# Zero writes moved to the routing, the row's owner word stored with the row, and an earlier schedule for weights, gathers and scaling in a two-network mixture-of-experts kernel

## The chip, the cores and the metric

The kernel runs on one core of one Trainium2 chip. The metric is the device time of one execution in microseconds (us). The engines are TensorE (PE, with its weight loads as PEld), VectorE (DVE), ScalarE (ACT), GpSimd (POOL) and SyncE (SP); SP, ACT and POOL issue DMA transfers, which run on 16 DMA engines.

## What is computed

A two-dimensional Fourier transform over 8 x 3072 tokens of 256 columns, of which the real part is kept; then a mixture of 8 experts whose weights P come from eight Sinkhorn iterations over all tokens; then a second mixture in which each token goes to its best expert alone.

```python
X = np.fft.fft(np.fft.fft(x, axis=1), axis=2).real          # (8, 3072, 256), then flattened
P = np.exp(logits - logits.max())                           # logits = X @ w_gate
for _ in range(8):
    P /= P.sum(1, keepdims=True) + 1e-09
    P /= P.sum(0, keepdims=True) + 1e-09
    P *= N / E
out = sum(P[:, e:e+1] * (np.maximum(X @ w1[e], 0) @ w2[e]) for e in range(8))
# second mixture: expert_idx = argmax(out @ w_gate2), its softmax weight, the same two layers
```

## The kernel before

Most tokens have a weight of zero for every expert after the exponential, so the kernel computes only the (token, expert) pairs that count. After the transform, a routing step (`route1`) finds them, sorts them into 30 tiles of 128 rows and gives each row's source index `R["hidx"]` and output row `R["ow"]`. Each of the 8 experts (e0 to e7) has CAP = 3 tiles of its own (t = 3e to 3e+2); NFLAT = 6 "free" tiles f0 to f5 hold what overflows, and one of them is computed in each of e2 to e7 with weights gathered per row (`Free.weights`: fw, the first layer, with rawc and gd, the second layer and gate). The rows are gathered from H by GpSimd, three gathers to a block (`grab`, L1335), ten blocks: one for each expert and two (8 and 9) for the free tiles. Between two gathers of blocks after the first two stand two memsets of a small tile, which space them.

Every product is done with each operand split into a high part and a low part: `part` (L813) has ScalarE copy a weight's high part (w1h, w2h) and VectorE subtract it for the low part (w1l, w2l); `relu` does the same for the hidden layer (hh, hl), `turn` (L840) for the transposed input (xh, xl). `build` in `moe1` (L1581) makes an expert's input x from the gathered rows in four steps a to d, with a, c and d on VectorE and b on ScalarE.

The order of the work is written by hand. `experts` walks through e0 to e7. In each there are slots: 0 to 7 after the eight pieces of the first layer, 8 to 10 in the free tile's second layer (from e2 on), 11 after the transposes of the next x, and 12 to 20, three in each of the second layer's tiles. Tables at L1431 to L1457 put pieces of other work into the slots: BUILD and FBUILD the steps a to d, PART the weight splits, ZERO the zero writes of the output (`zeros(2)` is one transfer of 512 KB), LOGIT the gate logits of a gathered block, GRAB1 the gathers, FREE the free weights, and SINK with STEPS the 18 Sinkhorn steps (start; eight times rows and column sums; end), where the k-th entry is counted in slots from SINK on. Each engine takes its instructions in that program order. The column sums are one matmul on TensorE (L999), which waits for the row step on VectorE. At the last step the weights are known: `add` then scales the stored tiles y and writes them to the accumulator `acc`, and `send` scatters with addition the rows that belong to another tile's owner; ADDS and SENDS give their slots. Before the weights are known, y is kept unscaled; at the end `ask` reads the second gate's logits back from acc.

Loads of whole weights go through three buffers rawa, rawb and rawc on SyncE's queue, in the order of the list FETCH; a load waits until the buffer's last reader is done, and what stands behind it on SyncE waits too. `fill` (L1310) places gate matmuls and other work inside `route1`; the string table G2 holds its letters: g a half of one expert's gate matmuls, l the write of L, digits the first splits, w a warming matmul. `azero` (L1612) writes zeros to the first rows of acc and then the output-row words, the column DG of acc.

Of the kernel before, what the change touches and what calls it, by code (L numbers as in the profile page):

```python
# [7 lines left out]
F32 = mybir.dt.float32  # L8
# [3 lines left out]
AF = mybir.ActivationFunctionType  # L12
# [1014 lines left out]
def dense(tc, ctx, A, K, rt, R, Ld, H, Pd, out, wg2):  # L1027
# [69 lines left out]
    with tc.For_i(0, NT, 1) as i:  # L1097
# [17 lines left out]
        for s in range(2):  # L1115
# [26 lines left out]
FETCH = [("t", 0, "a"), ("t", 1, "b"), ("t", 2, "c"), ("t", 3, "1"), ("t", 4, "2"), ("t", 5, "2"), ("w1", 0, "a"), ("w2", 0, "b"),  # L1142
         ("t", 6, "c"), ("t", 7, "a"), ("w2", 1, "b"), ("w1", 1, "a")]
FETCH += [(w, e, b) for e in range(2, E) for w, b in (("w1", "a"), ("w2", "b"))]
# [5 lines left out]
def run(tc, ctx, A, out, H, acc, Ld, Pd, Gd, Zd):  # L1150
# [62 lines left out]
    with tc.manual_schedule():  # L1213
# [27 lines left out]
        with ExitStack() as st:  # L1241
# [53 lines left out]
            with ExitStack() as s1:  # L1295
# [14 lines left out]
                def fill(k):  # L1310

                    def f():
                        for c in G2[k]:
                            if c == "g":
                                e, q = half.pop(0)
                                gates2(e, [q])
                            elif c == "l":
                                nc.sync.dma_start(out=Ld, in_=L.rearrange("p t s e -> p (t s e)"))
                            elif c == "w":
                                warm(1)  # L1320
                            else:
                                part("w", 0, int(c), nc.vector, lows[int(c) // 2])
                    return f
# [11 lines left out]
                def grab(j):  # L1335
                    X[j] = xg.tile([128, CAP, HW], F32, name="Xg")
                    for i in range(CAP):
                        t = CAP * j + i
                        if j > 1:

                            for _ in range(2):
                                nc.gpsimd.memset(grow, 0.0)
                        gather(nc, X[j][:, i], H[0:12296], R["hidx"][:, t:t + 1])
# [94 lines left out]
ONP, ONQ, ONB = [], [(7, 5)], ()  # L1438
FREE = {"w": 5, "u": 2}

BUILD = [(5, 7, 7, 11), (0, 1, 2, 3), (1, 2, 3, 4), (0, 1, 2, 3), (0, 1, 2, 3), (1, 2, 3, 4), (3, 4, 4, 5), (1, 2, 3, 4)]
FBUILD = ((1, (11, 12, 14, 15), 0), (4, (11, 12, 12, 15), 0))
ZERO = [(4, 11, 15), (4, 11, 16), (4, 11, 16), (4, 11, 16), (2, 11, 16), (2, 11, 16), (2, 11, 16), (2,)]
LOGIT = ((0, 11), (0, 11), (0, 13), (0, 19), (1, 3), (1, 7), (1, 14), (1, 19), (0, 16), (2, 3))

GRAB1 = ((0, 0, 2), (0, 5, E), (0, 13, 3), (0, 18, 4), (1, 2, 5), (1, 7, 6), (1, 15, 7), (1, 20, E + 1))
SINK = (2, 4)
STEPS = [0, 0, 4, 4, 8, 8, 12, 12, 16, 16, 20, 20, 24, 24, 28, 28, 32, 33]
FIRST = 7
ADDS, SENDS = (1, 3, 5, 7, 9, 13, 14, 15, 17, 19), (7, 13, 16, 19)  # L1450

GRAB = ((0, 17, 4), (1, 4, 5), (2, 4, 9), (2, 14, 6), (3, 13, 7))
PROB = ((0, 4, 0), (0, 1, 1), (1, 11, 8), (2, 6, 2), (3, 4, 3), (4, 4, 4), (4, 11, 9), (5, 4, 5), (6, 4, 6), (7, 5, 7))
BACK, BF, BL = [(8,), (8,), (8,), (8,), (4, 8), (2, 4, 6, 8)], ((2, 9), (4, 9), (6, 9)), 10
G2 = ("gg", "", "gggggg", "0l12g3gg", "ggww", "ggg")
Y2 = (8, 9)
# [86 lines left out]
class Free:  # L1543
# [5 lines left out]

    def weights(self, f):  # L1550
        moe = self.moe
        for i in range(2 + (self.Gd is not None)):
            if i < 2:
                t = (moe.fp, moe.raw)[i].tile([128, 2, FF], F32, name=("fw", "rawc")[i])
                d = t.rearrange("p k f -> p (k f)")
            else:
                t = moe.fp.tile([128, 8, 8], F32, name="gd")
                d = t.rearrange("p a b -> p (a b)")
            gather(self.nc, d, self.src[i], self.R["frow"][:, f:f + 1])
            self.w[f, i] = t  # L1560
# [14 lines left out]
def moe1(nc, K, R, acc, moe, W, part, X, xg, Gd, w1f, w2f, xb, pt, zeros, zt, rest, ask, trash, warm, grow):  # L1575
# [35 lines left out]

    def azero():  # L1612

        ow = xb.tile([128, NTL + 1], F32, name="ow")
        o.cp(ow[:, 0:1], trash)
        o.cp(ow[:, 1:NFLAT + 1], R["ow"][:, E * CAP:])
        o.cp(ow[:, NFLAT + 1:], R["ow"][:, :E * CAP])
        n = (NFLAT + 1) * DW
        av = acc[:n // DW * 128].rearrange("(p a) d -> p (a d)", p=128)
        for c in range(0, n, 512):  # L1620
            w = min(512, n - c)
            nc.sync.dma_start(out=av[:, c:c + w], in_=zt[:, 0, :w])
        nc.sync.dma_start(out=acc.rearrange("(t p) c -> p t c", p=128)[:, :, DG], in_=ow)

# [3 lines left out]
    def keep(t, p):  # L1628
        y = late["y"].tile([128, DW], F32, name="y")
        if not alone(t):  # L1630
            G.memset(y[:, DG:], 0.0)
        nc.scalar.activation(out=y[:, :DG], in_=p, func=AF.Copy, **({"scale": R["wt"][:, t:t + 1]} if known[0] else {}))
        ys.append((t, y, p if known[0] else None))

    def add():

        if ys:
# [3 lines left out]
            if t < E * CAP:  # L1641
                r = row_tile(t) * 128
                late["q"].dma_start(out=acc[r:r + 128, :DG], in_=y[:, :DG])
                if not alone(t):
# [30 lines left out]
    for (e, at, g), j in zip(FBUILD, (E, E + 1)):  # L1675
        for s, f in zip(at, build(j, G if g else V)):
            sl.at(e, s, f)
    sl.at(0, 14, azero)
    for e, s, j in GRAB1:
# [30 lines left out]
    for f in range(NFLAT):  # L1710
        sl.at(F0 + f - 1, FREE["w"], lambda f=f: free.weights(f))
    turned, steps = experts(moe, W, "w", xt, lambda j: (lambda i: x[j][:, i]), sl, DG, keep, part, free, on, grow)
# [104 lines left out]
```

## Time and profile before

| | |
|---|---|
| median of 3 runs | 688.7 us (684.64 to 691.24) |
| profiled execution, its own time | 690.08 us |
| its span | 687.8 us |
| TensorE, VectorE, ScalarE, GpSimd busy | 636.7, 435.5, 323.9, 216.2 us |
| mean granted TensorE clock | 0.953 |

A row of a timeline gives the start and the length in us, the engine, the line, the operation, output<-input, and in brackets the idle time of that engine just before it with what ended the wait. Equal neighbours are merged, with their number behind an x. A row of a stretch gives the busy time of each engine in it, the granted clock of TensorE (1.00 is 2.4 GHz, 0.50 is 1.2 GHz), the busy share of the 16 DMA engines and the GB/s that they moved. Busy times count overlapping instructions once; an idle engine that is not the bottleneck costs nothing.

### The profile page before, as it was taken

The page shows a single profiled execution, that of the slowest core. Times are in us where ns is not written, and L with a number is a line of the kernel's source. Part 1 is how long each engine was busy: PE and PEld are TensorE (multiplying, and loading weights), DVE is VectorE, ACT ScalarE, POOL GpSimd, SP SyncE. Part 2 cuts the span into 40 slices and gives each one's busy share as a digit, 9 for nine tenths or more (in the row PEclk, how much of TensorE's full clock was granted, in tenths as well). Part 3 has the DMA queues.
Part 4 walks back from the last instruction along what each step waited for, and adds up shares of the span by engine and source line. Part 5 has one row for each costly group of instructions (what it writes and reads, how often), then busy time and mean ns, then how long its engine had stood idle before and what let it go on. Part 6 is the DMA issues. An engine that isn't in the chain of part 4 may idle for free. (4 is left out here: it accounts for less than half of the span.)

```text
span 687.8 us, 12757 instructions
## 1 busy us (share of the span) xinstructions
PE 636.7 (93%) x4835; PEld 612.8 (89%) x4835; DVE 435.5 (63%) x973; ACT 323.9 (47%) x696; POOL 216.2 (31%) x343
## 2 busy tenths in 40 slices
PE   9999999999998997996969896998799999999995
PEld 6889999999988996995959896997499999999995
DVE  3677877777238956759896671855466546745750
ACT  3444545555545213553434571763145555654651
POOL 0002221122110088821011513402367676332232
PEclk9989999999999779898989998999899999999999
DMA  8999998999889148897547879776654385457501
GB/s 212 274 220 289 258 292 271 271 294 298 305 294 372 63 130 277 304 236 282 184 156 188 248 198 363 201 255 190 198 195 167 116 307 220 181 190 262 207 24 35
DMA packets 63840, 155.24 MB, mean 226 GB/s; under 512 B 14788, under 2 KB 32588, under 8 KB 55965
## 3 DMA queue, kind: packets, MB, share of 16 engines
q1 hardware_dynamic: 53612, 114.54, 53.5%
q0 software_dynamic: 9840, 39.45, 17.9%
q8 instruction: 40, 0.66, 0.4%
q10 hardware_dynamic: 320, 0.37, 0.2%
q14 instruction: 28, 0.22, 0.1%
HBM read 103.90 MB, written 50.34 MB: 224 GB/s over the span
## 5 line engine op out<-in xcount | busy, mean ns | idle before, releaser
L431 DVE SCALAR_TENSOR_TENSOR hl<-ph,hh 128x384 fp32r<-128x384 f32 (+1 forms) x164 | 86.0, 543 | 105.7 <-ACT hh L880 105.3
L927 PE MATMUL py<-w2h,hh 128*128 128x264 f32 (+1 forms) x480 | 140.4, 292 | 0.0
L927 PE MATMUL py<-w2l,hh 128*128 128x264 f32 (+1 forms) x480 | 137.7, 287 | 0.0
L927 PE MATMUL py<-w2h,hl 128*128 128x264 f32 (+1 forms) x480 | 137.5, 287 | 0.0
L880 ACT ACTIVATE hh<-ph 128x384 fp32r<-128x384 f32 (+1 forms) x164 | 76.7, 481 | 60.8 <-PE ph L940 33.3
L927 PEld LDWEIGHTS py<-w2l,hh 128*128 128x128 f32 x480 | 93.0, 194 | 0.2 <-DVE w2l L832 0.2
L927 PEld LDWEIGHTS py<-w2h,hh 128*128 128x128 f32 x480 | 93.0, 194 | 0.0
L927 PEld LDWEIGHTS py<-w2h,hl 128*128 128x128 f32 x480 | 92.5, 193 | 0.0
L894 PE MATMUL ph<-xh,w1h 128*128 128x384 f32 x256 | 67.6, 345 | 1.1 <-DVE nf L426 0.9
L894 PE MATMUL ph<-xl,w1h 128*128 128x384 f32 x256 | 65.2, 335 | 0.0
L894 PE MATMUL ph<-xh,w1l 128*128 128x384 f32 x256 | 65.1, 335 | 0.0
L126 POOL TENSOR_TENSOR lc<-hd 128x32 f32<-128x32 f32 (+1 forms) x25 | 9.5, 381 | 167.6 <-ACT hd L122 149.8
L74 PE MATMUL pp<-ca,w 96*128 96x96 f32 x512 | 61.5, 279 | 0.0
L74 PEld LDWEIGHTS pp<-ca,w 96*128 96x128 f32 x512 | 60.4, 196 | 0.8 <-issue 0.3
L801 POOL DMA_INDIRECT out_dram<-y,Rorow x30 | 33.2, 1108 | 82.0 <-ACT hh L880 26.9
L940 PE MATMUL ph<-Xg,fw 128*128 128x128 f32 x384 | 47.3, 283 | 7.2 <-DMA fw<-in_w_dram,Rfrow 7.2
L940 PEld LDWEIGHTS ph<-Xg,fw 128*128 128x128 f32 x384 | 46.0, 199 | 7.6 <-DMA fw<-in_w_dram,Rfrow 5.6
L894 PEld LDWEIGHTS ph<-xh,w1h 128*128 128x128 f32 x256 | 45.4, 189 | 3.4 <-DVE nf L426 1.2
L91 PE MATMUL pp<-cb,t 128*128 128x128 f32 x368 | 47.5, 276 | 0.6 <-DVE t L84 0.6
L76 ACT ACTIVATE at<-pp 128x384 f32<-128x384 f32 x64 | 31.1, 492 | 33.3 <-PE pp L74 32.8
L894 PEld LDWEIGHTS ph<-xh,w1l 128*128 128x128 f32 x256 | 46.4, 188 | 0.0
L894 PEld LDWEIGHTS ph<-xl,w1h 128*128 128x128 f32 x256 | 46.3, 188 | 0.0
(332 smaller groups left out, 1266.2 us busy)
## 6 DMA issues: line engine op xcount, KB each, us to landing
out_dram<-zt SPq DMA_DIRECT2D x48, 512.0 KB
H<-hd SPq DMA_DIRECT2D x24, 562.0 KB
xa<-in_xa_dram SPq DMA_DIRECT2D x32, 384.0 KB
xm<-in_xm_dram SPq DMA_DIRECT2D x32, 384.0 KB
rawa<-in_w_dram SPq DMA_DIRECT2D x8, 1024.0 KB
rawb<-in_w_dram SPq DMA_DIRECT2D x8, 1024.0 KB
rawa<-in_u_dram SPq DMA_DIRECT2D x8, 1024.0 KB
rawb<-in_u_dram SPq DMA_DIRECT2D x8, 1024.0 KB
```

Source lines behind the costliest of these rows:

```text
L74: nc.tensor.matmul(p[:M, i], lhs(4 * h + i), ca, start=True, stop=True)
L76: nc.scalar.activation(out=at[:M, :, :, s0:s0 + 4], in_=p[:M].rearrange("m s g j -> m g j s"), func=AF.Copy)
L91: nc.tensor.matmul(p[:M, i * 128:(i + 1) * 128], t[:, i, :M], cb[:, (g0 + i) * 128:(g0 + i + 1) * 128], start=True, stop=True)
L126: nc.gpsimd.tensor_tensor(out=lc[:np_, :n], in0=hd[:np_, :, 129:137], in1=hd[:np_, :, 273:281], op=ALU.add)
L431: self.nc.vector.scalar_tensor_tensor(out, a, s, b, op0, op1)
L801: nc.gpsimd.indirect_dma_start(out=dst, out_offset=bass.IndirectOffsetOnAxis(ap=idx, axis=0), in_=src, in_offset=None, **kw)
L880: self.nc.scalar.activation(out=a[:, :n], in_=p[:, :n], func=AF.Relu)
L894: self.nc.tensor.matmul(p[:, :N], w, xx, start=(i == 0), stop=(i == 5))
L927: self.nc.tensor.matmul(p[:, :nd], c, W[2 + m // 4][w][:, m % 4, :nd], start=(m == 0 and i == 0), stop=(m == 7 and i == 2))
L940: self.nc.tensor.matmul(p[:, m * 128:(m + 1) * 128], w[:, k, (m0 + m) * 128:(m0 + m + 1) * 128], x[:, k, i * 128:(i + 1) * 128], start=(k ...
```

## The change

The output's zeros that e0 and e1 wrote (six transfers of 512 KB) and the zeros of acc are issued inside the routing, with a new letter z in `fill`. `azero` becomes `owners`, which writes the output-row words of 8 tiles only; the other tiles carry the word in column DG of y, put there by ScalarE in `keep`, and store it with the row. The first weight of e1 is loaded ahead of its second. Gathers of blocks 2 to 9 are no longer spaced by memsets and stand in earlier slots. The free weight's first layer is gathered in slot 1, the other two pieces stay in slot 5. The Sinkhorn steps begin in slot 13 of e1 and have five slots for each iteration; LOGIT follows. The sends stand in slots 7, 10, 13 and 16.

```diff
-         ("t", 6, "c"), ("t", 7, "a"), ("w2", 1, "b"), ("w1", 1, "a")]
+         ("t", 6, "c"), ("t", 7, "a"), ("w1", 1, "a"), ("w2", 1, "b")]
...
+                            elif c == "z":
+                                for _ in range(6):
+                                    zeros(2)
+                                n = (NFLAT + 1) * DW
+                                av = acc[:n // DW * 128].rearrange("(p a) d -> p (a d)", p=128)
+                                for a in range(0, n, 512):
+                                    w = min(512, n - a)
+                                    nc.sync.dma_start(out=av[:, a:a + w], in_=zt[:, 0, :w])
...
-                        if j > 1:
-
-                            for _ in range(2):
-                                nc.gpsimd.memset(grow, 0.0)
                         gather(nc, X[j][:, i], H[0:12296], R["hidx"][:, t:t + 1])
...
-FREE = {"w": 5, "u": 2}
+FREE = {"w": (1, 5), "u": 2}
-BUILD = [(5, 7, 7, 11), (0, 1, 2, 3), (1, 2, 3, 4), ...
+BUILD = [(5, 6, 6, 6), (0, 1, 2, 3), (1, 2, 3, 4), ...
-ZERO = [(4, 11, 15), (4, 11, 16), (4, 11, 16), (4, 11, 16), (2, 11, 16), (2, 11, 16), (2, 11, 16), (2,)]
-LOGIT = ((0, 11), (0, 11), (0, 13), (0, 19), (1, 3), (1, 7), (1, 14), (1, 19), (0, 16), (2, 3))
-GRAB1 = ((0, 0, 2), (0, 5, E), (0, 13, 3), (0, 18, 4), (1, 2, 5), (1, 7, 6), (1, 15, 7), (1, 20, E + 1))
-SINK = (2, 4)
-STEPS = [0, 0, 4, 4, 8, 8, 12, 12, 16, 16, 20, 20, 24, 24, 28, 28, 32, 33]
+ZERO = [(), (), (4, 11, 16), (4, 11, 16), (2, 11, 16), (2, 11, 16), (2, 11, 16), (2,)]
+LOGIT = ((0, 11), (0, 11), (0, 13), (0, 19), (1, 1), (1, 3), (1, 5), (1, 7), (0, 16), (1, 12))
+GRAB1 = ((0, 0, 2), (0, 2, E), (0, 5, 3), (0, 7, 4), (0, 13, 5), (0, 16, 6), (0, 19, 7), (1, 1, E + 1))
+SINK = (1, 13)
+STEPS = [0, 1, 8, 8, 13, 13, 18, 18, 23, 23, 28, 28, 33, 33, 38, 38, 43, 44]
-ADDS, SENDS = (1, 3, 5, 7, 9, 13, 14, 15, 17, 19), (7, 13, 16, 19)
+ADDS, SENDS = (1, 3, 5, 7, 9, 13, 14, 15, 17, 19), (7, 10, 13, 16)
-G2 = ("gg", "", "gggggg", "0l12g3gg", "ggww", "ggg")
+G2 = ("gg", "", "gggggg", "0lz12g3gg", "ggww", "ggg")
...
-    def azero():
-        ow = xb.tile([128, NTL + 1], F32, name="ow")
+    def owners():
+        ow = xb.tile([128, E], F32, name="ow")
         o.cp(ow[:, 0:1], trash)
-        o.cp(ow[:, 1:NFLAT + 1], R["ow"][:, E * CAP:])
-        o.cp(ow[:, NFLAT + 1:], R["ow"][:, :E * CAP])
...
+        o.cp(ow[:, 1:], R["ow"][:, CAP:E * CAP:CAP])
+        av = acc.rearrange("(t p) c -> p t c", p=128)[:, :, DG]
+        r = row_tile(CAP)
+        nc.sync.dma_start(out=av[:, 0:1], in_=ow[:, 0:1])
+        nc.sync.dma_start(out=av[:, r:r + CAP * (E - 1):CAP], in_=ow[:, 1:])
...
-        if not alone(t):
+        if t < E * CAP and not alone(t):
             G.memset(y[:, DG:], 0.0)
+        else:
+            nc.scalar.activation(out=y[:, DG:], in_=R["ow"][:, t:t + 1], func=AF.Copy)
...
-                late["q"].dma_start(out=acc[r:r + 128, :DG], in_=y[:, :DG])
+                w = DW if alone(t) else DG
+                late["q"].dma_start(out=acc[r:r + 128, :w], in_=y[:, :w])
...
-    sl.at(0, 14, azero)
+    sl.at(0, 14, owners)
...
-        sl.at(F0 + f - 1, FREE["w"], lambda f=f: free.weights(f))
+        sl.at(F0 + f - 1, FREE["w"][0], lambda f=f: free.weights(f, (0,)))
+        sl.at(F0 + f - 1, FREE["w"][1], lambda f=f: free.weights(f, (1, 2)))
```

## Rows read from the trace of the kernel before

**Rows 1.** The page: the span, and each engine's busy time.

```profile
span 687.8 us, 12757 instructions
PE 636.7 (93%) x4835; PEld 612.8 (89%) x4835; DVE 435.5 (63%) x973; ACT 323.9 (47%) x696; POOL 216.2 (31%) x343
```

**Rows 2.** Busy time by stretch: e2 and e3 (PE, PEld, DVE, ACT, POOL, clock, DMA, GB/s).

```profile
299.40:333.30 33.90, 27.38 (x192) 26.96 (x190) 27.41 (x70) 14.58 (x31) 3.04 (x5) 0.90 0.78 265
333.30:367.80 34.50, 27.93 (x194) 27.12 (x193) 29.51 (x75) 14.24 (x30) 3.12 (x5) 0.90 0.61 196
```

**Rows 3.** Timeline of TensorE, 250 to 430 us: instructions with idle time before them.

```profile
273.97 0.90 PE L847 MATMUL pt<-ident,x 128*128 128x128 f32 x3 [4.28 <-DVE x L1584]
...
319.03 0.60 PE L999 MATMUL pt<-cs,tri 128*128 128x8 f32 x2 [6.50 <-DVE cs L437]
347.77 0.39 PE L999 MATMUL pt<-cs,tri 128*128 128x8 f32 x2 [2.01 <-DVE cs L437]
353.31 0.55 PE L847 MATMUL pt<-ident,x 128*128 128x128 f32 x3 [1.80 <-DVE cs L428]
356.62 0.59 PE L999 MATMUL pt<-cs,tri 128*128 128x8 f32 x2 [2.76 <-DVE xl L422]
394.95 3.81 PE L940 MATMUL ph<-Xg,fw 128*128 128x128 f32 x32 [1.75 <-DMA fw<-in_w_dram,Rfrow]
424.79 5.84 PE L940 MATMUL ph<-Xg,fw 128*128 128x128 f32 x32 [5.43 <-DMA fw<-in_w_dram,Rfrow]
```

**Rows 4.** After the wait in e0: one stretch, and e1's first matmul.

```profile
274.00:278.00 4.00, 4.00 (x19) 4.00 (x20) 3.86 (x20) 0.57 (x2) 3.18 (x6) 0.50 0.59 95
...
279.46 0.52 PE L894 MATMUL ph<-xh,w1h 128*128 128x384 f32 x2
```

**Rows 5.** The chain that ended last: start, length, what; two pieces at full clock.

```profile
438.96 2.91 PE py L927 x24
...
536.90 3.57 PE ph L940 x32
```

**Rows 6.** Timelines of SyncE and ScalarE: e1's first weight, issued and used.

```profile
259.17 0.52 SPq L1210 DMA_DIRECT2D rawa<-in_w_dram  x1
...
271.13 2.00 ACT L824 ACTIVATE w1h<-rawa 128x1024 fp32r<-128x1024 f32 x2 [6.18 <-DMA rawa<-in_w_dram]
```

**Rows 7.** Timeline of VectorE, e2: a logits step's end, start's first, row step's last.

```profile
309.49 0.19 DVE L422 TENSOR_TENSOR P<-P,sg__3013 128x24 f32<-128x24 f32 x1
...
314.23 0.28 DVE L434 COPY vp<-Rvalid 128x24 f32<-128x24 f32 x2
...
318.40 0.58 DVE L437 TENSOR_REDUCE cs<-P 128x8 f32<-128x240 f32 x1
```

**Rows 8.** Timelines of VectorE and TensorE in e1: the build of block 8.

```profile
281.31 0.56 DVE L431 SCALAR_TENSOR_TENSOR hl<-ph,hh 128x384 fp32r<-128x384 f32 x1 [2.96 <-ACT hh L880]
...
294.29 0.55 DVE L1584 TENSOR_TENSOR Xg<-Xg 128x381 f32<-128x381 f32 x1
...
294.09 0.52 PE L874 MATMUL pt<-ident,Xg 128*128 128x128 f32 x3
```

**Rows 9.** Timeline of GpSimd: first and seventh scatter; the chain: the gather behind.

```profile
372.21 1.62 POOL L801 DMA_INDIRECT acc<-y,Rapos  x1 [25.70 <-DMA acc<-y]
...
412.63 1.55 POOL L801 DMA_INDIRECT acc<-y,Rapos  x1 [3.43 <-ACT w1h L824]
...
414.48 10.26 DMA fw<-in_w_dram,Rfrow
```

**Rows 10.** A stretch of the routing, columns as in rows 2.

```profile
226.00:238.00 12.00, 11.52 (x101) 10.88 (x100) 11.79 (x16) 2.65 (x6) 0.00 (x0) 0.85 0.01 3
```

**Rows 11.** Timelines of GpSimd and VectorE: the third gather, its use, the spacing memsets.

```profile
243.49 0.95 POOL L796 DMA_INDIRECT Xg<-H,Rhidx  x1 [0.30 <-issue]
...
247.04 0.30 DVE L1584 TENSOR_TENSOR Xg<-Xg 128x33 f32<-128x33 f32 x2 [0.60 <-DMA Xg<-H,Rhidx]
...
250.17 0.66 POOL L1342 MEMSET grow<- 8x256 f32 x2
```

More of the change, by code (lines that the diff above doesn't have):

```diff
@@ L1438 @@
 ONP, ONQ, ONB = [], [(7, 5)], ()
-FREE = {"w": 5, "u": 2}
-BUILD = [(5, 7, 7, 11), (0, 1, 2, 3), (1, 2, 3, 4), (0, 1, 2, 3), (0, 1, 2, 3), (1, 2, 3, 4), (3, 4, 4, 5), (1, 2, 3, 4)]
+FREE = {"w": (1, 5), "u": 2}
+BUILD = [(5, 6, 6, 6), (0, 1, 2, 3), (1, 2, 3, 4), (0, 1, 2, 3), (0, 1, 2, 3), (1, 2, 3, 4), (3, 4, 4, 5), (1, 2, 3, 4)]
 FBUILD = ((1, (11, 12, 14, 15), 0), (4, (11, 12, 12, 15), 0))
-ZERO = [(4, 11, 15), (4, 11, 16), (4, 11, 16), (4, 11, 16), (2, 11, 16), (2, 11, 16), (2, 11, 16), (2,)]
-LOGIT = ((0, 11), (0, 11), (0, 13), (0, 19), (1, 3), (1, 7), (1, 14), (1, 19), (0, 16), (2, 3))
-GRAB1 = ((0, 0, 2), (0, 5, E), (0, 13, 3), (0, 18, 4), (1, 2, 5), (1, 7, 6), (1, 15, 7), (1, 20, E + 1))
-SINK = (2, 4)
-STEPS = [0, 0, 4, 4, 8, 8, 12, 12, 16, 16, 20, 20, 24, 24, 28, 28, 32, 33]
+ZERO = [(), (), (4, 11, 16), (4, 11, 16), (2, 11, 16), (2, 11, 16), (2, 11, 16), (2,)]
[3 more added lines that the diff above has]
+STEPS = [0, 1, 8, 8, 13, 13, 18, 18, 23, 23, 28, 28, 33, 33, 38, 38, 43, 44]
 FIRST = 7
-ADDS, SENDS = (1, 3, 5, 7, 9, 13, 14, 15, 17, 19), (7, 13, 16, 19)
+ADDS, SENDS = (1, 3, 5, 7, 9, 13, 14, 15, 17, 19), (7, 10, 13, 16)
 GRAB = ((0, 17, 4), (1, 4, 5), (2, 4, 9), (2, 14, 6), (3, 13, 7))
@@ L1548, in __init__, with weights @@
         self.w, self.w2, self.x = {}, {}, {}
-    def weights(self, f):
+    def weights(self, f, pieces=(0, 1, 2)):
         moe = self.moe
-        for i in range(2 + (self.Gd is not None)):
+        for i in pieces[:len(pieces) if self.Gd is not None else 2]:
             if i < 2:
@@ L1609, in build @@
         return [a, b, c, d]
-    def azero():
-        ow = xb.tile([128, NTL + 1], F32, name="ow")
+    def owners():
+        ow = xb.tile([128, E], F32, name="ow")
         o.cp(ow[:, 0:1], trash)
-        o.cp(ow[:, 1:NFLAT + 1], R["ow"][:, E * CAP:])
-        o.cp(ow[:, NFLAT + 1:], R["ow"][:, :E * CAP])
[L1618 to L1623, printed above, removed]
+        o.cp(ow[:, 1:], R["ow"][:, CAP:E * CAP:CAP])
[3 more added lines that the diff above has]
+        nc.sync.dma_start(out=av[:, r:r + CAP * (E - 1):CAP], in_=ow[:, 1:])
     ys, sq, known, late = [], [], [False], {"q": nc.sync}
```

## The prediction

> **What bounds the kernel now.** I read the page first. The profiled execution spans 687.8 us and took 690.08 us, 2.3 us lying around the span; TensorE is busy for 93% of it and VectorE for 63% [rows 1]. So the kernel is bound by TensorE where TensorE is fed, and a change is worth what it takes from TensorE's waits. The change touches the routing and the first expert network, so the next view is the busy time by expert (e0 to e7): e2 takes 33.9 us and e3 34.5 us, while TensorE works 27.4 and 27.9 us in them and VectorE 27.4 and 29.5 us [rows 2]. VectorE has as much to do there as TensorE, so any order in which one waits for the other costs time. Then TensorE's own list of idle times says which wait ends last where [rows 3]. In e0 it stands 4.28 us for the tile x of e1, which VectorE builds. In e2 and e3 it stands four times, 6.50 + 2.01 + 1.80 + 2.76 = 13.1 us, for VectorE's Sinkhorn steps and what is queued around them (three of the four are the column-sum matmul of line 999). At the start of e5 and e6 it stands 1.75 and 5.43 us for a free tile's gathered weight fw. Together that is 24.5 us.
>
> A wait costs more than itself. After the 4.28 us wait the granted clock is 0.50 [rows 4], the lower of its two levels, and from 273.97 to 279.46 us TensorE needs 5.49 us for three transposes and 24 matmuls [rows 3, 4]. 24 such matmuls take 2.91 us at the full clock [rows 5], three transposes about 0.3, so 2.25 us more are lost. After the 5.43 us wait, 32 matmuls of line 940 take 5.84 us [rows 3] against 3.57 at the full clock [rows 5], so 2.27. I use 2.25 us for a drop of the clock. In e2 and e3 the mean clock is 0.90 each [rows 2]: one drop in each.
>
> **Part A, e0: weight order and build slots.** VectorE is late for x because it stands in program order behind the split of e1's first weight (w1l), and that behind ScalarE's w1h, which sat 6.18 us until the load landed at 271.1; SyncE had issued that load at 259.17 [rows 6], after the w2 load that waits for VectorE. The swap in FETCH issues w1 of e1 as soon as the gate matmuls have read its buffer, ahead of that wait, some 10 us sooner. BUILD[0] moreover puts both halves of x ahead of the split (slot 6, split at 7). The 4.28 us and the 2.25 us of clock go: 6.5 us gained. Bounds: nothing, if the load still lands late and x with it, up to 6.5.
>
> **Part B, e1: the Sinkhorn start moved into it.** SINK and LOGIT put three things into VectorE's queue in e1 ahead of the second half of x for the first free block (FBUILD slot 15): start with its first row step, in slots 13 and 14, and two more logits than before. Start and first row step run from 314.23 to 318.98 = 4.75 us; a logits step is three instructions, the last of 0.19 us [rows 7], overlapping: 0.4 us, 0.6 at most. Sum 4.75 + 0.8 = 5.6. VectorE is nearly gapless in e1: its first instruction there is at 281.31, the last of that build at 294.29, and TensorE begins the transposes of that block at the same moment, 294.09 [rows 8]. So nothing covers the addition; I allow half a microsecond for small idle times. A wait of 5.1 us appears at line 874, followed by transposes and an expert tile at the low clock: I take one drop, 2.0. Cost 7.1 us. Bounds: 3 (the wait broken by the first three transposes, no drop) to 7.9.
>
> **Part C, e2 and e3.** What was moved leaves here: start, first row step and one logits, 4.75 + 0.4 = 5.2 us of VectorE work out of a stretch in which VectorE ends the waits. Each later iteration (column scaling and row step) has five slots instead of four, but the last still ends in slot 15 of e3 instead of 16, so the total otherwise stays. TensorE's waits go from 13.1 to about 7.5 us: a few of 1 to 3 us, at the column sums in slots 10 of e2 and 14 of e3 above all. With waits that short I expect one of the two clock drops to stay away. Gain 5.6 + 2.0 = 7.6. Bounds: 3 (the work is only shifted, both drops remain) to 13.1 + 4.5 = 17.6, if every wait went; I take the row of the work removed, for VectorE's other work in e2 and e3 is untouched.
>
> **Part D, e5 and e6.** GpSimd's queue holds scatters and gathers in one order. Before, seven scatters precede the weight gather of e6's block (two at slot 16 and one at 19 of e3, four in e4); they run from 372.21 to 412.63, 6.7 us apart, each waiting for the one before, and the gather issued behind them at 414.48 takes 10.26 us to land [rows 9]. After, SENDS and the new place of the known step leave two in e3 and four in e4: six, and fw is gathered in slot 1. As GpSimd is behind its slots, slot 1 or 5 matters little; the one scatter fewer does. The gather lands near 424.75 - 6.7 = 418.0, TensorE wants it at 419.36 less the 1.75 us that go from e5: 417.6. A wait of 0.5 to 1.5 stays, none at e5. Gain 1.75 + 5.43 + 2.27 - 1.0 = 8.4. Bounds: 2 (the scatters are paced by the transfers and the gather is as late as before) to 9.45.
>
> **Edits at nothing.** The zeros at the routing: six output zeros (3.15 MB) and the four of acc (0.95 MB). From 226 to 238 us the DMA engines are empty, share 0.01 [rows 10]; at 340 GB/s (265 at a share of 0.78 [rows 2]) 4.1 MB take 12.1 us, just the hole. SyncE has no other transfer to issue in that hole, so its queue is covered too. Were the cover gone, the last gate weights and the first row gathers behind them would be late by what overhangs, 0 to 3 us. The owner words: one DMA of 3968 words of 4 bytes becomes one of 1024, and 23 y tiles get a ScalarE copy of one column, each well under the 1.0 us of a copy of 1024 columns [rows 6]; ScalarE works 47% of the span [rows 1] and no wait of TensorE's in rows 3 is for it. The DMA engines full of small words in e1 held back no load that TensorE waited for: 0. The spacing memsets: two take 0.66 us on GpSimd; without them a gather is issued every 0.95 + 0.30 = 1.25 us, as the first six already are [rows 11], with them every 1.8. The 24 of the experts then take 30 us and not 43. No wait of TensorE's is for them; the price of a late one is a rival below.
>
> **Sum.** + 6.5 - 7.1 + 7.6 + 8.4 = 15.4 us. 690.08 - 15.4 = 674.7 us. The profiled execution lies 1.4 us above the median of the runs (688.7); by the median it would be 673.3.
>
> **Rivals.**
> *Work only moves (13%).* VectorE's full queue in e0 to e3 is what counts, and spreading it gives little: C is 3, B its upper 7.9, D 5. 6.5 - 7.9 + 3 + 5 = 6.6: 683.5. For it speaks VectorE's load above TensorE's in e2 and e3 [rows 2]; against it, that VectorE idles in e0 for the late weight [rows 6], time which part A hands it.
> *GpSimd stays as late, or the early weight isn't early (17%).* The edits don't do what they are for: fw(4) still lands 10 us behind a scatter chain, D is 2; or w1 of e1 still lands at 271, A is 0. Either gives 681 (9.0 or 8.9 gained). For it speaks the 10.26 us landing, a transfer limit and not a queue's [rows 9].
> *No new wait in e1 (12%).* VectorE gets through start early, B costs 1.5, and C gains 9.5: 22.9 gained, 667.2.
> *A late gather stops VectorE: slower (8%).* The logits of the tenth block stand in e1 slot 12, in VectorE's queue ahead of everything of part B. Its three gathers are the last of 24. If unspaced gathers slow each other down, VectorE stands there, and TensorE behind it. They begin near 249, after the first six and ahead of the memsets' row at 250.17 [rows 11], so at 1.25 us the last is issued near 279 and lands near 283, by the third of the first six, which VectorE waited for from its issue at 243.49 to 247.04 [rows 11]. The slot is due near 285: e1 begins at 273 and the build behind the slot ended 14.8 us after e1's start before [rows 4, 8]. All 15.4 us are lost when the last lands near 301, at a pitch of 2.0 us; at 2.2 us it is some 695. Against it: six unspaced gathers already run at 1.25 us beside a busy VectorE [rows 11], and the zeros are gone from that stretch. The Trainium skill (SBUF — State Buffer, "SBUF: two separate sides") has a rule for such a thing: a VectorE instruction in a two-port mode shuts GpSimd out of the shared port, so that it can't write descriptors and its DMA starves. By that rule the gathers would stretch where VectorE copies in SBUF; the gather's row, 0.95 us while VectorE works, does not show it.
>
> **How the numbers follow.** Forecast 50% (670 to 681), the others as given. The range leaves out the slower case (8%), the far half of the first rival (to 687) and a tail under 667: 667 to 684. What a measurement here can tell from no change is about 1%, 6.9 us. By the median, faster by over 1% is below 681.8: 50 + 12 + 10 of the 17 = 72%. Within 1%: the other 7 and 13 = 20%. Slower: 8%.
>
> **What would show it.** A: no idle time at the transposes of line 847 in e0, e1's first matmul near 273. B: an idle time of about 5 us at line 874 in e1, for VectorE. If it is absent, B is wrong. C: idle at line 999 in sum about 7 us in e2 and e3. D: idle before line 940 at e5 none, at e6 about 1 us. The zeros: DMA share near 1 between 226 and 238, gate matmuls and first transposes where they are. It is wrong as a whole if VectorE waits for a gather (logits), if e0 begins later than before, or if e2 begins before 294, which would mean that VectorE had room in e1.

## The result, and the profile after

The changed kernel takes 682.6 us (median of 20 runs, 678.5 to 687.3), the kernel before 690.4 us beside it (20 runs, 684.6 to 694.8): ratio 0.988, 95% interval 0.986 to 0.990. That is 7.7 us or 1.2% faster. The profiled execution of after took 679.7 us, 2.9 us less than its median, while that of before (690.1) is at its median. So the two profiles differ by 10.4 us, and 2.7 of these are the choice of the execution: differences of stages below are larger than those of the medians.

The page of after, the span and the busy times [rows 1 of before]:

```profile
span 677.3 us, 12712 instructions
PE 635.4 (94%) x4835; PEld 612.9 (90%) x4835; DVE 435.4 (64%) x972; ACT 326.6 (48%) x719; POOL 203.8 (30%) x289
```

The work is the same on TensorE and VectorE; what is gone is waiting. Busy time by stretch, after: e0, e1, e2, e3, e4 (start to end, length, then PE, PEld, DVE, ACT, POOL busy, granted clock, DMA share, GB/s), to be held against [rows 2]:

```profile
252.50:273.10 20.60, 19.03 (x126) 17.69 (x127) 17.68 (x64) 8.87 (x21) 16.25 (x15) 1.00 0.71 216
273.10:299.90 26.80, 21.51 (x134) 20.56 (x133) 18.09 (x56) 12.95 (x30) 8.78 (x10) 0.87 0.67 216
299.90:333.60 33.70, 28.40 (x194) 27.27 (x192) 25.74 (x60) 14.70 (x33) 2.93 (x4) 0.90 0.52 164
333.60:364.30 30.70, 26.91 (x191) 26.47 (x190) 26.74 (x67) 14.50 (x33) 2.93 (x4) 0.94 0.61 202
364.30:389.80 25.50, 25.14 (x190) 24.82 (x189) 17.43 (x36) 16.25 (x38) 10.36 (x7) 1.00 0.86 251
```

And TensorE's instructions with idle time before them in e1 to e6, against [rows 3] (the longest):

```profile
291.01 0.52 PE L874 MATMUL pt<-ident,Xg 128*128 128x128 f32 x3 [2.97 <-DVE Xg L1588]
293.51 0.87 PE L874 MATMUL pt<-ident,Xg 128*128 128x128 f32 x3 [1.98 <-DVE Xg L1588]
310.62 0.63 PE L894 MATMUL ph<-xh,w1h 128*128 128x384 f32 x2 [1.51 <-DVE hl L431]
320.45 0.60 PE L999 MATMUL pt<-cs,tri 128*128 128x8 f32 x2 [2.71 <-DVE cs L437]
322.59 0.90 PE L847 MATMUL pt<-ident,x 128*128 128x128 f32 x3 [0.81 <-DVE cs L428]
353.55 0.90 PE L847 MATMUL pt<-ident,x 128*128 128x128 f32 x3 [3.53 <-DVE cs L428]
414.91 3.84 PE L940 MATMUL ph<-Xg,fw 128*128 128x128 f32 x32 [0.72 <-DMA fw<-in_w_dram,Rfrow]
```

The 4.28 us of e0 are gone. New are 4.95 us at line 874 in e1, both for VectorE's build of the free block. Of the four waits of e2 and e3 there are 2.71, 0.81 and 3.53 left, beside some small ones (1.51, 0.27, 0.26): 9.1 us in place of 13.1. TensorE doesn't wait at e5, and 0.72 us at e6. Only 2.97 us (2.71 and 0.26) of this is at the column sums of line 999; 4.34 us stand at the transposes of line 847 and 1.51 us at line 894.

Cut at TensorE's first matmul of each expert, the whole comes out as this (us; e6 here reaches to the next run of line 940). A wait ahead of an expert's first matmul falls into the expert before it: the waits at e5 and e6 are in the columns e4 and e5.

| | start | e0 | e1 | e2 | e3 | e4 | e5 | e6 | rest |
|---|---|---|---|---|---|---|---|---|---|
| before | 253.2 | 26.3 | 19.9 | 34.0 | 34.4 | 27.2 | 29.8 | 37.5 | 225.5 |
| after | 252.5 | 20.6 | 26.8 | 33.7 | 30.7 | 25.5 | 25.1 | 35.6 | 226.8 |
| gain | 0.7 | 5.6 | -6.9 | 0.3 | 3.7 | 1.7 | 4.8 | 2.0 | -1.3 |

### The profile page after: what moved, and what is told of

Its sections match the earlier page's. It is cut to its first block, busy times and chain, and to the rows that moved or that the text cites. A ratio compares the mean times of both kernels' runs of the same rounds, so it can differ in the third digit from the quotient of the medians.

```text
span 677.3 us, 12712 instructions
## 1 busy us (share of the span) xinstructions
PE 635.4 (94%) x4835; PEld 612.9 (90%) x4835; DVE 435.4 (64%) x972; ACT 326.6 (48%) x719; POOL 203.8 (30%) x289
## 4 chain that ended last, share of the span: by engine, by line
PE 49%; DMA 9%; DVE 8%; issue 2%; ACT 2%; POOL 0%; SPq 0%; POOLq 0%; ACTq 0%; DVEq 0%
PE py L927 21%; PE ph L894 15%; PE ph L940 6%; PE py L1256 3%; DVE hl L431 2%; DMA out_dram<-zt 2%; PE pt L847 2%; DMA fw<-in_w_dram,Rfrow 2%; DVE w2l L830 1%; DMA acc<-zt 1%; DMA acc<-y,Rapos 1%; PE py L1275 1%; DVE w1l L830 1%; DMA Xg<-acc,Rgidx 1%; DMA rawa<-in_w2t_dram 1%
## 5 line engine op out<-in xcount | busy, mean ns | idle before, releaser
L940 PE MATMUL ph<-Xg,fw 128*128 128x128 f32 x384 | 45.2, 275 | 0.7 <-DMA fw<-in_w_dram,Rfrow 0.7
L91 PEld LDWEIGHTS pp<-cb,t 128*128 128x128 f32 x368 | 44.4, 192 | 0.9 <-DVE t L84 0.8
```

The source lines that it names most:

```text
L91: nc.tensor.matmul(p[:M, i * 128:(i + 1) * 128], t[:, i, :M], cb[:, (g0 + i) * 128:(g0 + i + 1) * 128], start=True, stop=True)
L940: self.nc.tensor.matmul(p[:, m * 128:(m + 1) * 128], w[:, k, (m0 + m) * 128:(m0 + m + 1) * 128], x[:, k, i * 128:(i + 1) * 128], start=(k ...
```

## The experiments

The runs fall on four chips, here A to D, each with runs of the kernel before beside them: 690.6 (A), 694.5 (B), 691.9 (C) and 692.4 us (D). Ratios are to these. Each run left one profile. The record doesn't name the chips of the two profiles above. The chip matters, as it turned out.

### Which edit clears e6 (chip A)

```
a_oldsends:  SENDS = (7, 13, 16, 19)      # was (7, 10, 13, 16)
a_slot5:     FREE = {"w": (5, 5), "u": 2} # was (1, 5)
```

> The changed kernel with SENDS (7, 13, 16, 19) as before in place of (7, 10, 13, 16). Theory: which scatters stand ahead of the gather of fw for e6 on GpSimd's queue sets e6's wait; with a later place there is either one more scatter ahead of the gather or the same number later, so a wait of 5 to 7 us is back at e6's first matmul, and part of the 2.3 us that the clock costs behind it: 5 to 8 us slower than the changed kernel, 688 to 690. Rival: the earlier slot of the gather is what cures the wait; then nothing changes, 682 to 683, and e6's wait stays under 1 us.

> The changed kernel with all pieces of the free weights asked for in slot 5 (FREE w (5, 5)) instead of the first in slot 1. Theory: GpSimd runs its queue late against TensorE's slots, so the slot matters only through the order of the instructions; the gather then stands behind the same scatters, lands within 1 us of where it did, and the time is that of the changed kernel, 682 to 683, with e5 without a wait and e6 with at most 1.5. Rival: the early slot is the cure; then 1.75 us come back at e5 and 5 us at e6, and the time is 687 to 690.

With the old SENDS: 689.4 us, ratio 1.001 (0.998 to 1.005). With slot 5: 682.4 us, ratio 0.990 (0.986 to 0.994). Timelines of a_oldsends, GpSimd's last scatter and the gather behind it, and TensorE at e6:

```profile
407.89 2.48 POOL L801 DMA_INDIRECT acc<-y,Rapos  x1 [3.30 <-ACT w1h L824]
410.68 1.01 POOL L796 DMA_INDIRECT fw<-in_w_dram,Rfrow  x1 [0.30 <-issue]
...
420.41 6.07 PE L940 MATMUL ph<-Xg,fw 128*128 128x128 f32 x32 [6.23 <-DMA fw<-in_w_dram,Rfrow]
```

And of a_slot5:

```profile
404.06 1.56 POOL L801 DMA_INDIRECT acc<-y,Roidx  x1 [2.92 <-ACT hh L880]
405.92 1.01 POOL L796 DMA_INDIRECT fw<-in_w_dram,Rfrow  x1 [0.30 <-PE py L927]
...
416.06 3.84 PE L940 MATMUL ph<-Xg,fw 128*128 128x128 f32 x32 [1.07 <-DMA fw<-in_w_dram,Rfrow]
```

With the old SENDS seven scatters stand ahead of this gather, with the new ones six; the gather is issued at 410.68 and not at 405.92, and e6 waits 6.23 us. Asking for the weight in slot 5 or slot 1 changes nothing, since GpSimd gets to it only after the same scatter. The gain is in SENDS, not in the gather's earlier slot.

### The Sinkhorn back at its old place (chip A)

```
SINK = (2, 4)                             # was (1, 13)
STEPS = [0, 0, 4, 4, 8, 8, ... 28, 28, 32, 33]
LOGIT = (... (1, 3), (1, 7), (1, 14), (1, 19), (0, 16), (2, 3))
```

> The changed kernel with the Sinkhorn's places of the kernel before (SINK, STEPS, LOGIT). Theory: moving it to e1 cost 6.9 us there and gave back 4.0 us in e2 and e3, so undoing it makes e1 20 us long, e2 and e3 34 us each again with 13 us of waits, and the whole some 3 us faster than the changed kernel: about 680 by the median. Rival: the earlier start is where the change's gain comes from; with the old places the time is 4 to 7 us longer, 687 to 690.

684.3 us, ratio 0.991 (0.987 to 0.994), where a_slot5, in effect the changed kernel, has 0.990 on the same chip. Neither theory's number came, and the stage lengths say why:

| | e0 | e1 | e2 | e3 | e0 to e4 | e4 | e5 |
|---|---|---|---|---|---|---|---|
| after | 20.6 | 26.8 | 33.7 | 30.7 | 111.8 | 25.5 | 25.1 |
| a_oldsink | 20.6 | 19.9 | 34.2 | 34.1 | 108.8 | 25.3 | 29.7 |

Up to e4 the old place is 3.1 us faster, just as 6.9 us of loss in e1 against 4.0 of gain in e2 and e3 had said. It is lost again in e5. Timelines of a_oldsink, first scatter, the weight gather, and TensorE at e6:

```profile
364.62 1.63 POOL L801 DMA_INDIRECT acc<-y,Rapos  x1 [25.57 <-DVE hl L431]
...
404.17 1.18 POOL L796 DMA_INDIRECT fw<-in_w_dram,Rfrow  x1 [0.30 <-PE py L927]
...
414.97 6.68 PE L940 MATMUL ph<-Xg,fw 128*128 128x128 f32 x32 [5.29 <-DMA fw<-in_w_dram,Rfrow]
```

After's own rows for the same two instructions on GpSimd:

```profile
366.27 1.62 POOL L801 DMA_INDIRECT acc<-y,Rapos  x1 [19.72 <-DMA acc<-y]
...
403.94 1.77 POOL L796 DMA_INDIRECT fw<-in_w_dram,Rfrow  x1 [0.30 <-issue]
```

Six scatters stand ahead of the gather in both, and it is issued at the same time. But e4 begins at 360.02 here and at 364.32 in after, so TensorE comes to e6 earlier and waits. Against the start of e4, the chain of scatters begins 4.6 us late here and 1.95 us in after, and the gather is issued at 44.15 and 39.62 us. Starting the Sinkhorn in e1 thus pays nothing on balance in e1 to e3; in these two profiles it is worth 4.6 us at e6.

That it does so by letting the scatters begin sooner is not shown. In c_zeros (below) the Sinkhorn stands where after has it and six scatters are ahead of the gather, the first of them 2.8 us after the start of e4 at 396.04. Yet the gather is issued 44.15 us after that start, as in a_oldsink, and e6 waits:

```profile
440.19 1.18 POOL L796 DMA_INDIRECT fw<-in_w_dram,Rfrow  x1 [0.30 <-PE py L927]
...
451.12 6.41 PE L940 MATMUL ph<-Xg,fw 128*128 128x128 f32 x32 [5.42 <-DMA fw<-in_w_dram,Rfrow]
```

In a_startlate (next) the first scatter is as late, 2.9 us, and the gather is issued at 39.7 us. So the pace of the scatters comes in two forms, and what chooses between them is open. By time, 0.991 and 0.990, the two places of the Sinkhorn can't be told apart.

### The Sinkhorn started behind the build, in e1's last slots (chip A, then C)

```
a_startlate:  SINK = (1, 16), first steps [0, 1, 5, 5, 10, 10, ...], three of the last four logits in (1, 15)
a_startlast:  SINK = (1, 18), first steps [0, 1, 3, 3, 8, 8, ...], logits as in a_startlate
```

> The changed kernel with the start of the Sinkhorn and its first row step taken from behind the first slots of e1 to its end (SINK (1, 16), first steps there), and the last four blocks' logits with it, behind the build of the free weight's block. Theory: in the changed kernel these steps stand in VectorE's queue ahead of the build that TensorE waits for at line 874 (2.97 and 1.98 us), while VectorE is idle for 5.0 and 2.2 us at the end of e1. Put behind the build they fill that idle time: both waits go (under 0.5 us left), the clock drop behind them (some 2 us) goes with them, e1 is 20 us long instead of 26.8, e2 and e3 keep their lengths (33.7 and 30.7), and the whole is 6 to 7 us faster than the changed kernel, about 676 by the median. Rival: VectorE's work, not its order, is what is short; the waits of e1 come back in e2 (e2 near 40 us) and the time stays at 681 to 684.

a_startlate took 680.5 us, ratio 0.988 (0.980 to 0.997), from four runs of 675.5, 676.5, 684.5 and 685.0: too far apart to tell it from the changed kernel by time. Its profile is 675.5 us; its span of 672.9 is 4.4 us under after's. By stage the theory holds: e1 is 21.2 us instead of 26.8, e2 33.5 and e3 30.6 as in after, e6 waits 0.59. Both waits at line 874 are gone, and the rival (they come back in e2) is refuted. One wait is left, at TensorE's transposes behind (ScalarE first, then TensorE):

```profile
288.71 0.50 ACT L950 ACTIVATE P<-P,bias 128x240 f32<-128x240 f32 x1 [4.15 <-DVE bias L949]
289.47 0.86 ACT L875 ACTIVATE Xg<-pt 128x384 f32<-128x384 f32 x2
...
290.00 0.93 PE L847 MATMUL pt<-ident,x 128*128 128x128 f32 x6 [2.33 <-ACT Xg L875]
```

The start has an exponential on ScalarE. It stood there for VectorE's bias, and the eviction of line 875, which TensorE wants, stood behind it.

> As the run with the Sinkhorn's start in e1 slot 16, but from slot 18 (SINK (1, 18)), the row steps of e2 and e3 left in the slots they had there. Theory: in that run TensorE still waited 2.33 us at line 847, because the exponential of the start stood in ScalarE's queue ahead of the eviction of the free block's transposes (line 875) and waited there for VectorE; two slots later it stands behind both evictions, the wait goes, e1 is 20 us long, e2 to e6 as in that run, and the time is 1.5 to 2.5 us below it: ratio to the kernel before 0.978 to 0.986 against 0.988 of the changed kernel. Rival: VectorE is then late with the first row step or the split of tile 2 (line 422), and the 2 us come back in e2.

a_startlast took 707.2 us, ratio 1.022 (1.016 to 1.027), far off both theories, for a reason that lies ahead of e0 (below). Behind that place its stages are as the theory has them: e1 19.1 us, e2 33.6, e3 30.6, e6's wait 0.93. ScalarE's order in it, eviction first:

```profile
317.44 0.87 ACT L875 ACTIVATE Xg<-pt 128x384 f32<-128x384 f32 x2
318.56 0.87 ACT L850 ACTIVATE xh<-pt 128x384 fp32r<-128x384 f32 x2 [0.26 <-PE pt L847]
320.57 0.50 ACT L950 ACTIVATE P<-P,bias 128x240 f32<-128x240 f32 x1 [1.13 <-DVE bias L949]
```

### A wider pitch of the row steps (chip C)

```
SINK = (1, 18); STEPS = [0, 1, 3, 3, 9, 9, 15, 15, ... 39, 39, 45, 46]   # every 6 slots, not 5; logits as in a_startlast
```

> The same with a row step every 6 slots instead of every 5, so that fewer of them lie in e2 and e3 and the Sinkhorn ends in e4 slot 1 instead of e3 slot 15. Theory: what is left of waits in e2 and e3 (5.3 and 3.8 us in the changed kernel) is VectorE's load in these two experts, which a wider pitch takes down: e2 and e3 together 3 to 6 us shorter; but the scatters can't begin before the Sinkhorn ends, some 7 slots or 9 us later against TensorE, and the gathers of the free weights stand behind them: 5 to 12 us of waits come back at e5 and e6, and the whole is 2 to 6 us slower than with a pitch of 5. Rival: the scatters' pace is set by their own landings and has slack, the waits at e5 and e6 stay under 2 us, and it is faster by 3 to 6 us.

717.2 us, ratio 1.036 (1.029 to 1.042), with the same loss ahead of e0; against a_startlast, on the same chip, 10 us slower, where 2 to 6 were expected. Its e2, e3, e4 and e5 take 32.8, 31.6, 29.7 and 30.1 us, those of a_startlast 33.6, 30.6, 25.5 and 25.3. So e4 and e5 pay 9 us. The 4.8 of e5 are the later scatters, as expected: e6 waits 5.71 us for its gather. The 4.2 of e4 are not: TensorE doesn't wait for a gather at e5, but 1.74 and 0.93 us in e4 for VectorE's split of the hidden layer (line 431), which now stands behind the Sinkhorn's last step and the scaling of the stored tiles, and the mean granted clock from 400 to 405 us is 0.71. And e2 and e3 are no shorter in sum (64.3 against 64.2 us): that half of the theory falls. What is left of waits there does not yield to a wider pitch.

### FETCH and BUILD one at a time, in the kernel before (chip B)

```
b_fetch:  ... ("t", 7, "a"), ("w1", 1, "a"), ("w2", 1, "b")]
b_build:  BUILD = [(5, 6, 6, 6), ...      # was (5, 7, 7, 11)
```

> The kernel before with the fetch order of the change alone (w1 of expert 1 ahead of w2 of expert 1). Theory: the 4.28 us at the end of e0 come from VectorE standing behind ScalarE's wait for w1 of expert 1, which came last; with it fetched some 10 us sooner the x tiles of e1 are built in time even in the old build slots, the wait goes, and e1 begins at 273 in place of 279.5; 4 to 6.5 us by the middle of the program, of which e6's wait for the gather (which follows GpSimd's queue) takes part back at the end: 684 to 688. Rival: it is the build slots (5, 7, 7, 11) that hold the x tiles back; then nothing changes.

> The kernel before with the build slots (5, 6, 6, 6) of e0 alone. Theory: the x tiles of e1 are then in VectorE's queue ahead of the late weight, so the transposes at line 847 wait no more, but the first matmul of e1 needs that very weight, which lands as late as before: the wait moves from the transposes to e1's first matmul and nearly nothing is gained, 689 to 691. Rival: the slots are the cure, e1 begins at 273 and the time is 684 to 688.

b_fetch: 692.8 us, ratio 0.995 (0.991 to 0.9996). e0 is 19.6 us long instead of 26.3, so the weight order alone does part A; from e0's start to e6's this profile is 5.2 us shorter than that of before. b_build: 696.3 us, ratio 1.000 (0.996 to 1.005). Its e0 is 21.7 us, so the slots alone clear most of that wait too; my theory that it moves to e1's first matmul is wrong. There is a new wait instead in e2, which is 40.4 us long. ScalarE, VectorE and TensorE in e2 of b_build:

```profile
303.83 0.18 DVE L422 TENSOR_TENSOR sg__3013<-Xg 128x24 f32<-128x24 f32 x1 [6.61 <-DMA Xg<-H,Rhidx]
...
314.37 1.06 ACT L824 ACTIVATE w2h<-rawb 128x1024 fp32r<-128x1024 f32 x1 [5.39 <-DMA rawb<-in_w_dram]
315.46 1.23 DVE L830 TENSOR_TENSOR w2l<-rawb,w2h 128x1024 fp32r<-128x1024 f32 x1 [4.95 <-ACT w2h L824]
...
324.90 0.59 PE L999 MATMUL pt<-cs,tri 128*128 128x8 f32 x2 [11.41 <-DVE cs L437]
```

With e0 shorter, VectorE comes to the logits sooner than the gathers, which these two kernels still issue with spacing: the last at 298.4 us, 295.7 in the profile of before, where VectorE has no such idle time. But b_fetch has nearly the same idle time of VectorE at this place, 5.23 us, and its e2 is 34.4 us long with a wait of 6.39 at line 999, as in before (6.50). So the late gather is not what makes e2 long in b_build. What b_fetch doesn't have is the other wait: ScalarE stands 5.39 us for the second weight of e2, VectorE behind it 4.95, and the Sinkhorn's start behind that. The load was issued at 296.83 there and at 293.28 in b_fetch, whose ScalarE doesn't wait for it. With FETCH changed, the shorter e0 is thus kept even with spaced gathers.

### The spacing, and the zeros (chips B and C)

```
c_spaced:    if j > 1: for _ in range(2): nc.gpsimd.memset(grow, 0.0)   # back ahead of each gather
c_zeros:     G2 without "z"; ZERO[0], ZERO[1] and acc's zeros as before
c_zeros_sp:  both
```

> The changed kernel with the two spacing memsets back ahead of every row gather behind the first six. Theory: the 24 gathers then come every 1.8 us in place of 1.25, the last lands near 294 to 297 in place of some 283, the logits of the last block (e1, slot 12) stand in VectorE's queue until then, and the build that TensorE waits for stands behind them: e1 is 6 to 10 us longer than in the changed kernel and the time 688 to 693. It puts a price on the rival that a late gather stops VectorE. Rival: the gathers have slack (VectorE is behind its slots anyhow) and the time stays at 682 to 684.

> The changed kernel with all zeros (six output zeros and those of acc) back at their places in e0 and e1 in place of the routing. Theory: they were put at nothing because no wait of TensorE's hangs on them; so the time stays within 1 us of the changed kernel's, 682 to 684, and the transfers of e0 and e1 get some longer only. Rival: the zeros share the DMA engines with the unspaced row gathers and the weights of e1, and a late gather or weight holds VectorE: 2 to 6 us longer, 685 to 688.

> The changed kernel with all zeros back in e0 and e1 and the spacing memsets back as well. With the zeros alone put back TensorE stood still for 27 us between its transposes in front of e0, until the last of the unspaced gathers was out, without a wait that the trace names. Theory: that standstill needs the unspaced gathers; with the memsets back it is gone, and the time is that of the changed kernel with the memsets alone, ratio to the kernel before 0.997 to 1.005. Rival: the zeros' place makes it, whatever the pitch of the gathers; the hole of more than 20 us stays, ratio above 1.02.

c_spaced: 694.9 us, ratio 1.000 (0.995 to 1.005), some 8 us above the changed kernel by the ratios, 6.7 of them in e1 (33.5 us against 26.8). The last gather is issued at 294.89, VectorE stands 5.99 us for one of the last, and behind VectorE TensorE:

```profile
296.74 0.18 DVE L422 TENSOR_TENSOR sg__3033<-Xg 128x24 f32<-128x24 f32 x1 [5.99 <-DMA Xg<-H,Rhidx]
...
303.67 0.87 PE L874 MATMUL pt<-ident,Xg 128*128 128x128 f32 x3 [9.30 <-DVE Xg L1591]
```

This is what the slower rival said of VectorE and TensorE, with a price: a pitch of 1.8 us takes the whole gain.

c_zeros: 717.4 us, ratio 1.031 (1.024 to 1.037), and neither theory had this. Its e0 to e4 are as long as after's within 0.5 us (20.9, 26.4, 33.4, 30.6, 25.3; e6 waits 5.42 us, as shown above). What is lost lies ahead of e0: TensorE stands still 27.21 us among the transposes, ahead of a warming matmul. c_zeros_sp: 693.5 us, ratio 1.001 (0.997 to 1.004), no such hole. So the standstill needs the unspaced gathers, and the zeros' place alone does not make it. a_startlast and a_wide, with the zeros at the routing, have it too, 27.28 and 27.19 us.

### The same kernel on another chip (chip D)

> The kernel of the run a_startlate once more, unchanged. In three kernels TensorE stood still for 27 us between the transposes ahead of e0 (zeros put back; start in slot 18; wide pitch); the last two differ from a_startlate only in e1 and later, behind the standstill. Theory: the standstill hangs on the chip: the three ran on two other chips than a_startlate did, and there the kernels with spaced gathers too lost some 1 to 4 us at that place. On such a chip this kernel stands still as well and takes 700 to 710 us, ratio to the kernel before 1.015 to 1.03. Rival: it hangs on the program (where its instructions lie); then this kernel, which had none, has none here either, whatever the chip: ratio 0.975 to 0.99, TensorE's first matmul of e0 near 252 to 257. On a chip like the first the two can't be told apart, and the run tells only how much the later start is worth: 0.977 to 0.986 if its profile (4.4 us below the changed kernel's) stands for its runs.

709.7 us, ratio 1.025 (1.020 to 1.030), on chip D, where on chip A the very same kernel had 680.5. Windows of it on D, then of the first run on A (columns as above):

```profile
249.00:253.00 4.00, 2.80 (x30) 2.29 (x29) 0.00 (x0) 0.00 (x0) 2.98 (x4) 0.83 0.43 119
253.00:281.00 28.00, 1.22 (x3) 0.70 (x4) 0.00 (x0) 0.20 (x1) 18.89 (x20) 0.50 0.55 155
```

```profile
249.00:253.00 4.00, 3.84 (x28) 2.76 (x29) 1.02 (x2) 0.87 (x2) 3.09 (x4) 1.00 0.95 283
253.00:281.00 28.00, 26.44 (x173) 25.40 (x172) 22.88 (x81) 15.06 (x35) 21.91 (x21) 1.00 0.80 207
```

On D TensorE works 1.22 us of the 28, VectorE nothing, ScalarE 0.20; GpSimd alone goes on, a gather every 1.25 us. TensorE's rows, and GpSimd's last gather:

```profile
256.38 0.59 PE L1275 MATMUL py<-zb 128*128 128x512 bf16 x1 [3.75 <-issue]
...
283.00 1.01 PE L1275 MATMUL py<-zb 128*128 128x512 bf16 x2 [25.18 <-remote]
```

```profile
276.94 0.95 POOL L796 DMA_INDIRECT Xg<-H,Rhidx  x1 [0.30 <-issue]
```

The standstill hangs on the chip, not on the program. (Each chip was used in one round of runs, so chip and round can't be told apart.) From the first gather's issue to e0's first matmul it takes 44.3 to 44.5 us in the four unspaced kernels on B, C and D, 14.4 to 14.9 in the four spaced ones on B and C, 12.4 in before and 12.6 in after, and no more than 13.2 in the four unspaced ones on A. In each of the four TensorE goes on 5.9 to 6.1 us after the last gather is issued, about when it has landed (the last one of b_build was waited for until 5.45 us after its issue).

## Why the prediction was right, and where it was not

The sign and the range (667 to 684) hold, but narrowly: the median of 682.6 lies 1.4 us inside the range's end, and by the medians half of the gain came (7.7 of 15.4 us). The forecast of 674.7 is 5.0 us under the profile of after and 8 under its median. Of the 4.9 us between 15.4 predicted and 10.5 in the spans, 3.6 are part C, 0.9 part A, and 1.3 were lost behind e6, which no run takes apart.

**Part A, 6.5 predicted, 5.6 measured.** Right in mechanism: FETCH alone gives it. SyncE issues the load 10.4 us sooner than in [rows 6], and ScalarE's w1h doesn't wait for it:

```profile
248.79 0.33 SPq L1210 DMA_DIRECT2D rawa<-in_w_dram  x1
...
263.32 2.00 ACT L824 ACTIVATE w1h<-rawa 128x1024 fp32r<-128x1024 f32 x2
```

That BUILD[0] helps beside it was half right: it frees the x tiles by itself, but in before the gain is lost again to the late weight in e2.

**Part B, 7.1 predicted, 6.9 measured.** Right in place (line 874), releaser (VectorE), wait (5.1 against 4.95) and clock. The window from 293 to 300 us has a mean granted clock of 0.59. a_startlate takes 5.6 of it back and a_startlast 7.7, by order alone: VectorE is idle 5.03 us at the end of e1, so the work fits into e1 and only its place in the queue was dear. The prediction saw no cover because it looked only ahead of the build.

**Part C, 7.6 predicted, 4.0 measured: the mis-sized term.** The step that failed is "TensorE's waits go from 13.1 to about 7.5 us" together with "I expect one of the two clock drops to stay away". 9.1 us of waits stayed, and not where it looked for them: 2.97 us at line 999 in place of about 7. Both drops stayed too: after 2.71 and after 3.53 us of waiting the granted clock is 0.50, the lower level, though in e3 for a shorter time (the mean of e3 is 0.94, before 0.90). After, two stretches in e2 and e3:

```profile
320.00:326.00 6.00, 4.74 (x21) 4.35 (x22) 5.76 (x14) 1.93 (x3) 0.00 (x0) 0.50 0.90 361
354.00:356.00 2.00, 2.00 (x11) 2.00 (x10) 1.83 (x6) 1.44 (x2) 0.00 (x0) 0.50 1.00 340
```

Of the 5.2 us of work taken off VectorE 4.0 came off the waits, and shorter waits were still followed by the lower clock. Why the rest of the waits stays is open; a wider pitch does not shorten it (a_wide). Together, B and C are a loss of 2.9 us in e1 to e3, and a_oldsink measures it as 3.1.

**Part D, 8.4 predicted, 8.4 measured** (1.7 + 4.8 + 2.0). The step holds: the count of scatters ahead of the gather matters (a_oldsends), the slot doesn't (a_slot5). But the count is not all: in a_oldsink and in c_zeros some 5 us of the wait stand although the count is six. So that the sum came out to the tenth is luck in part.

**Edits at nothing.** The hole of [rows 10] was used as foreseen: from 226 to 238 us the DMA engines' share is now 0.76 (288 GB/s), short of the "near 1" expected, and e0 begins no later. That the zeros cost nothing is borne out in part. In c_zeros e0 to e4 have the same lengths with them at either place, but e6 waits; with the spacing back as well (c_zeros_sp against c_spaced, on two chips) the ratios are 1.001 and 1.000, with e1 at 36.2 and 33.5 us. For the spacing memsets it fails twice. Their loss was priced only as a possible late gather; in fact the unspaced gathers are what keeps VectorE from waiting (c_spaced, 8 us). And on three of the four chips the unspaced gathers come with a standstill of TensorE.

**The slower rival (8%)** named the right edit, and by the estimate below it would have come true on three of the four chips, but by another mechanism than gathers that slow each other. They don't; they keep a pitch of 1.25 us on chip D too. The Trainium skill (SBUF — State Buffer, "SBUF: two separate sides") has VectorE, in some of its instructions, shut GpSimd out of a port that they share. The trace of after agrees with it in small: three of the gathers take 1.97, 1.34 and 1.76 us in place of 0.95, each issued at most 0.3 us behind the start of a VectorE TENSOR_TENSOR. The first:

```profile
255.02 1.21 DVE L830 TENSOR_TENSOR w2l<-rawb,w2h 128x1024 fp32r<-128x1024 f32 x1
255.09 1.97 POOL L796 DMA_INDIRECT Xg<-H,Rhidx  x1 [0.31 <-issue]
```

That is 2.2 us in all, far from the price of the rival, and it is not the standstill: in the hole on D VectorE's busy time is 0.00, each gather takes 0.94 or 0.95 us, and GpSimd goes on. The changed kernel itself was not run on B, C or D; a_startlate has the same instructions in the same order on TensorE and GpSimd and lost 29 us from A to D, so an estimate for the changed kernel there is 682 + 29 = 711 us, slower than before by nearly 3% and outside the range. The 29 us are uncertain by some 5, as the four runs of a_startlate on A lie between 675.5 and 685.0. The ratio of 0.988 is that of the chips on which the pair was timed.

## What to carry to other kernels

Before moving a step into an in-order queue, read what is waited for behind its new place, and where that queue is idle: here the same 5 us of VectorE work cost 7 us ahead of a build and nothing behind it. What a move gives or costs can show on another engine and later: in one profile the Sinkhorn's old place was 3.1 us ahead at e4 and had lost it to GpSimd's scatters at e6. Follow two kernels stage by stage to the end before a wait is put down to an edit, and look for the wait that only the slow one has: b_build and b_fetch share the idle time for a gather, and only one of them pays. Instructions that seem to do nothing but space others are not to be costed at nothing from one trace; time such a change on more than one chip where you can.

## What the runs showed of the hardware

While GpSimd issues 24 row gathers with a pitch of 1.25 us, TensorE and ScalarE can stand for 25 to 27 us with no wait that the trace names ("issue", "remote"), until about when the last gather has landed; with two memsets, 0.66 us together, between gathers (pitch 1.8) about 2 us are lost at that place on B and C. Chip A, and the chips on which before and after were profiled, show none of it. What TensorE waits for is open: the trace has no instruction of VectorE, ScalarE or SyncE that it could be, and no run took the cause apart further. A late fetch of instructions would be a rival, but the trace has no sign of it: in a_startlate_2 no packet of the two instruction queues (q8, q14) lies between 245 and 300 us, and TensorE goes on at 283.00 all the same; the run on A has three packets there. Whether a spacing between the two (one memset) would keep the early gathers without the standstill was not tried.

No version that ran beats both kernels on all chips: a_startlate is ahead of after by its profile on A (675.5 against 679.7) and behind before on D. b_fetch, which keeps the spacing, is ahead of before on B, one of the chips with the standstill, by 0.5%.
